# Weights of a convolution interleaved by four columns, and their products written in runs of 8 bytes

## The chip, the cores and the metric

One core of a Trainium2 chip. The metric is device time of one execution in microseconds (us), as a median over runs. Kernels are compared only within the same rounds.

## The reference, cut to what matters

Two independent blocks, concatenated: an attention block A and a long convolution B.

```python
# A: qkv = x @ wqkv, 32 heads of 16; softmax(q k^T * 16**-0.5) @ v; @ wo     (S = 2048, D = 512)
# B: per channel d (512 channels, 2048 positions):
k_shift = sum over t of k_pad[:, t:t + S, :] * shift_k[:, ks - 1 - t]        # 4 taps
kv      = k_shift * v                                                        # <- the products of this case
y       = causal convolution of kv with ssm_k (length S), done by FFT + kv * ssm_D
b       = q * y
```

The kernel does B's long convolution on TensorE: `kv` is the stationary operand (the weights), shifted rows of `ssm_k` are streamed. Two channels share the 128 rows (64 each), and four such pairs run side by side in four column groups of 32.

## The kernel before: the parts that matter

```python
KVF = sb("KV", [128, C // 2, 2, 2 * NB])                 # 256 columns u; 2 parities; 32 weights, contiguous
KV = KVF[:, :, :, :].rearrange("p u r (e h) -> p r e h u", h=2)
...
# one unit "kv": 32 matmuls in two halves into one PSUM bank (L360), then VectorE empties it with two products (L399)
for p in range(2):
    dst = KV[64 * p:64 * p + 64, i // 4, 4 * (i % 4):4 * (i % 4) + 4, p, 128 * c:128 * c + 128]
    val = VST[64 * p:64 * p + 64, c, i // 4, 4 * (i % 4):4 * (i % 4) + 4, :]
    src = PS[64 * p:64 * p + 64, bank, :].rearrange("p (b d) -> p b d", b=4)
    h_kvc[c] = hh = urgent(lambda e, dst=dst, src=src, val=val: e.tensor_tensor(dst, src, val, ALU.mult),
                           [h, h_vn[2 * c + i // 4], h_kv0], us=V512)
bank_free[bank] = hh                                     # the next unit's matmuls wait for the second product
...
# the convolution (L814): for each of 32 lags, four column groups
for c in range(4):
    ins = e.matmul(PS[32 * c:32 * c + 32 - 2 * q, BGB, 128 * kk:128 * kk + w],
                   lhsT=KVF[:, 4 * od + c, lag % 2, 2 * q:32],       # 2 to 32 weights, side by side
                   rhs=WR[:, rows[c], w0:w0 + w], start=(n == 0), stop=(n == NLAG - 1), tile_position=(0, 32 * c))
```

Around this runs the attention. For each score step, TensorE makes two or three blocks of scores (L546), ScalarE exponentiates them (L557), and VectorE takes over one of the three blocks of some steps (L593, L600, L605: some 3.4 us of work each). TensorE also sums with the values (L639). Program order is fixed on each engine before anything runs: of the 13388 matmuls in the traces before and after, 13314 stand at the same place in the order of start. There are 741 score steps with a ScalarE exponential. Below, "step n" is the n-th of them in a trace, so the same piece of work can be found in every trace.

The softmax here doesn't subtract the row's maximum and nothing guards it: scores larger than these inputs give would overflow.

## Time and profile before

1052.42 us (median of 2 runs, 1052.06 to 1052.78). The profiled run lasted 1056.7 us.

| view of the kernel before | value |
|---|---|
| busy share of TensorE, VectorE, ScalarE | 81%, 81%, 81% |
| products L399: number, mean, sum | 32, 2444 ns, 78.2 us |
| share of L399 in the chain that ended last | 7.4% of 1054.9 us, so 78 us |
| stage of the products, steps 60 to 180 (84.7 to 293.4 us): length, mean PE clock | 208.7 us, 0.65 |

Three engines at 81% say little: the share is an average over stages with different limits. The row to read is the third: a group's whole busy time lies on the chain. The lines themselves stand in the prediction.

### The profile page before, as it was taken

The page shows a single profiled execution, that of the slowest core. Times are in us where ns is not written, and L with a number is a line of the kernel's source. Part 1 is how long each engine was busy: PE and PEld are TensorE (multiplying, and loading weights), DVE is VectorE, ACT ScalarE, POOL GpSimd, SP SyncE. Part 2 cuts the span into 40 slices and gives each one's busy share as a digit, 9 for nine tenths or more (in the row PEclk, how much of TensorE's full clock was granted, in tenths as well). Part 3 has the DMA queues.
Part 4 walks back from the last instruction along what each step waited for, and adds up shares of the span by engine and source line. Part 5 has one row for each costly group of instructions (what it writes and reads, how often), then busy time and mean ns, then how long its engine had stood idle before and what let it go on. Part 6 is the DMA issues. An engine that isn't in the chain of part 4 may idle for free.

```text
span 1054.9 us, 29610 instructions
## 1 busy us (share of the span) xinstructions
PE 854.8 (81%) x13388; PEld 333.1 (32%) x13388; DVE 851.4 (81%) x1330; ACT 858.4 (81%) x746; POOL 31.1 (3%) x34
## 2 busy tenths in 40 slices
PE   7987786887788788888788888897788878888877
PEld 2222222233233333333333333333333333333322
DVE  3239898898888798888797968788798879898892
ACT  5896674765598898888797978788799869898897
POOL 7000000000000000000000000000000000000000
PEclk9897585866589898899898978779999879898899
DMA  9940001321498798898787888978778778788602
GB/s 252 246 85 1 1 1 40 81 46 37 103 198 197 164 202 187 197 195 191 155 187 175 185 176 199 235 170 194 168 179 183 163 166 183 178 185 177 139 2 60
DMA packets 68013, 155.14 MB, mean 147 GB/s; under 512 B 31152, under 2 KB 33200, under 8 KB 67504
## 3 DMA queue, kind: packets, MB, share of 16 engines
q1 hardware_dynamic: 62624, 145.12, 62.6%
q0 software_dynamic: 1808, 6.29, 2.1%
q8 instruction: 106, 1.74, 0.8%
q10 hardware_dynamic: 3456, 1.84, 0.6%
q14 instruction: 19, 0.16, 0.1%
HBM read 142.61 MB, written 6.42 MB: 141 GB/s over the span
## 4 chain that ended last, share of the span: by engine, by line
PE 37%; ACT 31%; DVE 21%; issue 8%; DMA 2%; SPq 1%; ACTq 0%; DVEq 0%
ACT PT L557 31%; PE PS L546 13%; PE PS L639 8%; PE PS L814 8%; DVE KV L399 7%; DVE EH L600 6%; DVE FX L593 3%; PE PS L360 2%; DVE PTD L605 2%; DMA WR<-kz_scratch 2%; PE PS L339 2%; PE PS L1019 1%; PE PS L756 1%; SPq L222 1%; DVE DT L703 1%
## 5 line engine op out<-in xcount | busy, mean ns | idle before, releaser
L557 ACT ACTIVATE PT<-PS 128x1536 bf16<-128x1536 f32 (+1 forms) x741 | 855.3, 1269 | 183.9 <-PE PS L546 180.5
L546 PE MATMUL PS<-QT,KTo 32*128 32x512 bf16 x2048 | 347.0, 436 | 85.0 <-ACT PT L557 43.7
L814 PE MATMUL PS<-WR,KV 128*30 128x128 bf16 (+8 forms) x8192 | 265.1, 237 | 47.5 <-issue 40.7
L600 DVE SCALAR_TENSOR_TENSOR EH<-EH,FX 128x512 f32<-128x512 f32 x426 | 280.5, 678 | 0.4
L639 PE MATMUL PS<-PT,VAF 128*32 128x512 bf16 x1835 | 233.4, 443 | 17.4 <-DVE DT L703 8.0
L814 PEld LDWEIGHTS PS<-WR,KV 128*18 128x18 bf16 (+7 forms) x8192 | 173.9, 97 | 157.7 <-issue 125.9
L593 DVE TENSOR_SCALAR FX<-PS 128x512 f32<-128x512 f32 x213 | 145.9, 685 | 70.6 <-PE PS L546 69.9
L546 PEld LDWEIGHTS PS<-QT,KTo 32*128 32x128 bf16 x2048 | 75.1, 93 | 279.5 <-ACT PT L557 158.6
L605 DVE SCALAR_TENSOR_TENSOR PTD<-EH,FX 128x512 uint16<-128x512 f32 x213 | 143.6, 678 | 0.2
L600 DVE SCALAR_TENSOR_TENSOR EH<-FX 128x512 f32<-128x512 uint16 x213 | 141.5, 681 | 0.1
L639 PEld LDWEIGHTS PS<-PT,VAF 128*32 128x32 bf16 x1835 | 51.0, 95 | 163.5 <-issue 140.8
L1019 PE MATMUL PS<-IDN,ZW 128*32 128x512 bf16 (+3 forms) x243 | 83.4, 343 | 4.1 <-issue 4.1
L399 DVE TENSOR_TENSOR KV<-PS,WR 64x512 bf16<-64x512 f32 x32 | 78.2, 2444 | 8.5 <-PE PS L360 8.0
L639 PE MATMUL PS<-PTD,VAF 128*32 128x512 bf16 x213 | 71.5, 448 | 2.2 <-issue 2.2
L703 DVE STREAM_TRANSPOSE DT<-PS 128x512 f32<-128x512 f32 x31 | 22.1, 712 | 32.6 <-PE PS L639 32.4
L412 DVE CAST VAF<-PS 128x512 bf16<-128x512 f32 x16 | 11.1, 691 | 31.7 <-PE PS L368 31.7
L385 DVE TENSOR_SCALAR QT<-PS,MASK 128x512 bf16<-128x512 f32 x30 | 21.1, 745 | 14.6 <-PE PS L339 14.4
L1019 PEld LDWEIGHTS PS<-IDN,ZW 128*32 128x32 bf16 x243 | 25.2, 104 | 8.9 <-issue 8.9
L339 PE MATMUL PS<-xT,WQ 128*128 128x512 bf16 x60 | 24.6, 507 | 3.1 <-DVE KV L399 2.2
L360 PE MATMUL PS<-OTN,QN 128*64 128x128 bf16 x256 | 14.9, 285 | 13.6 <-DVE KV L399 13.5
L360 PE MATMUL PS<-OTN,QT 128*64 128x128 bf16 x256 | 14.9, 285 | 12.7 <-DVE KV L399 12.6
L368 PE MATMUL PS<-WKV,xT 128*128 128x512 bf16 x64 | 21.1, 424 | 4.4 <-DVE VAF L412 4.0
(63 smaller groups left out, 237.1 us busy)
## 6 DMA issues: line engine op xcount, KB each, us to landing
WR<-kz_scratch SPq DMA_DIRECT2D x256, 512.0 KB, 8.7
kz_scratch<-WR SPq DMA_DIRECT2D x1, 2176.0 KB, 8.5
WR<-in_B_v_dram SPq DMA_DIRECT2D x8, 256.0 KB, 6.9
QN<-in_B_q_dram POOLq DMA_DIRECT2D x2, 1024.0 KB, 9.9
out_dram<-QN POOLq DMA_DIRECT2D x2, 1024.0 KB, 10.0
out_dram<-OUTA POOLq DMA_DIRECT2D x12, 128.0 KB, 5.3
QN<-in_B_ssm_k_dram SPq DMA_DIRECT2D x1, 1024.0 KB, 6.3
QT<-in_B_ssm_k_dram SPq DMA_DIRECT2D x1, 1024.0 KB, 8.2
```

Source lines behind the costliest of these rows:

```text
L339: return e.matmul(PS[:, bank, :], lhsT=WQ[:, dc, o * 128:(o + 1) * 128], rhs=xT[:, dc, qb * 512:(qb + 1) * 512], start=(dc == 0), stop=(dc ...
L360: ins = e.matmul(PS[64 * h:64 * h + 64, bank, 128 * b:128 * b + 128], lhsT=KTR[c][:, h, c0:c0 + 64], rhs=DG[:, 2 * c + h, m, :], start=(m ...
L399: h_kvc[c] = hh = urgent(lambda e, dst=dst, src=src, val=val: e.tensor_tensor(dst, src, val, ALU.mult), [h, h_vn[2 * c + i // 4], h_kv0], ...
L546: ins = e.matmul(PS[:, bank, :], lhsT=KTo[32 * s:32 * s + 32, g // 2, kt * 128:(kt + 1) * 128], rhs=QT[32 * s:32 * s + 32, qb % 2, g, :], ...
L557: h_exp[T] = act.op(lambda e: e.activation(PT[:, T % R_PT, 0:n * QB], PS[:, banks[0]:banks[0] + n, :].rearrange("p b f -> p (b f)"), ACT.E ...
L593: h_f = urgent(lambda e: e.tensor_scalar(fx, PS[:, bank, :], FIX_ADD, FIX_HI, ALU.add, ALU.min), [h, h_last.get(i - R_FX)], slack=0.6)
L600: st["h"] = dve.op(lambda e: e.scalar_tensor_tensor(eh, src, (A3, A2, A1)[j], frac, ALU.add, ALU.mult), [st["h"], h_last.get(i - R_EH), h_ ...
L605: lambda e: e.scalar_tensor_tensor(out16, eh, A4, fx, ALU.mult, ALU.add),
L639: ins = e.matmul(dst, lhsT=w, rhs=rhs, start=(k == 0), stop=(k == KT - 1), tile_position=(0, 32 * s))
L703: h_t = urgent(lambda e: e.transpose(out=dt, in_=PS[:, pvb(n), :]), [h] + before, slack=0.1, us=(0.63, 0.751))
L814: ins = e.matmul(PS[32 * c:32 * c + 32 - 2 * q, BGB, 128 * kk:128 * kk + w], lhsT=KVF[:, 4 * od + c, lag % 2, 2 * q:32], rhs=WR[:, rows[c] ...
L1019: pe.op(lambda e: e.matmul(PS[32 * s:32 * s + 32, pvb(n), 0:128 * k], lhsT=ZW[:, :], rhs=rhs, start=False, stop=False, tile_position=(0, 3 ...
```

## The change

The intent: no two consecutive elements of a product were neighbours in memory, so put four channels' columns next to each other and let the product write four of them in a row. The price is that the weights of one load then lie 8 bytes apart.

```diff
-    KVF = sb("KV", [128, C // 2, 2, 2 * NB])
-    KV = KVF[:, :, :, :].rearrange("p u r (e h) -> p r e h u", h=2)
+    KVF = sb("KV", [128, NOCT, 2, 2 * NB, 4])
+    KV = KVF[:, :, :, :, :].rearrange("p k r (e h) c -> p r e h k c", h=2)
 ...
-                dst = KV[..., p, 128 * c:128 * c + 128]
-                val = VST[...]
-                src = PS[64 * p:64 * p + 64, bank, :].rearrange("p (b d) -> p b d", b=4)
+                dst = KV[..., p, 32 * c:32 * c + 32, :].rearrange("p e k c -> p k e c")
+                val = VST[...].rearrange("p e (k c) -> p k e c", c=4)
+                src = PS[64 * p:64 * p + 64, bank, :].rearrange("p (e k c) -> p k e c", e=4, c=4)
 ...
-                                   lhsT=KVF[:, 4 * od + c, lag % 2, 2 * q:32],
+                                   lhsT=KVF[:, od, lag % 2, 2 * q:32, c],
```

("[...]" marks a cut: the indices there are those of before. The zero fill of the tile also got its fifth index.)

More of the change, by code (lines that the diff above doesn't have):

```diff
@@ L313, in bass_concat_heads__mha_block__ssm_conv_h3__prompt_kernel @@
     h_vaf1 = pool.op(lambda e: e.memset(VAF[:, :, H * VW:VROW], 1.0))
-    h_kv0 = pool.op(lambda e: e.memset(KVF[:, :, :, :], 0.0), [h_vaf1], us=(14.0, 14.1))
+    h_kv0 = pool.op(lambda e: e.memset(KVF[:, :, :, :, :], 0.0), [h_vaf1], us=(14.0, 14.1))
     h_kz0 = pool.op(lambda e: e.memset(KZS[:, :, S:S + PAD], 0.0), [h_kv0])
@@ L395, in evac_unit @@
             for p in range(2):
-                dst = KV[64 * p:64 * p + 64, i // 4, 4 * (i % 4):4 * (i % 4) + 4, p, 128 * c:128 * c + 128]
-                val = VST[64 * p:64 * p + 64, c, i // 4, 4 * (i % 4):4 * (i % 4) + 4, :]
-                src = PS[64 * p:64 * p + 64, bank, :].rearrange("p (b d) -> p b d", b=4)
+                dst = KV[64 * p:64 * p + 64, i // 4, 4 * (i % 4):4 * (i % 4) + 4, p, 32 * c:32 * c + 32, :].rearrange("p e k c -> p k e c")
+                val = VST[64 * p:64 * p + 64, c, i // 4, 4 * (i % 4):4 * (i % 4) + 4, :].rearrange("p e (k c) -> p k e c", c=4)
+                src = PS[64 * p:64 * p + 64, bank, :].rearrange("p (e k c) -> p k e c", e=4, c=4)
                 h_kvc[c] = hh = urgent(lambda e, dst=dst, src=src, val=val: e.tensor_tensor(dst, src, val, ALU.mult),
```

## The prediction

> **What bounds the kernel now.** I read four views: the groups by line (what the changed instruction costs), the chain of waits (whether that cost sets the end), that line's own view (who waits for it), and the busy times by stage (what could take its place).
>
> The groups by line, of the page; the columns are busy us and mean ns, then the idle time ahead and what ended it:
>
> ```profile
> L399 DVE TENSOR_TENSOR KV<-PS,WR 64x512 bf16<-64x512 f32 x32 | 78.2, 2444 | 8.5 <-PE PS L360 8.0
> L412 DVE CAST VAF<-PS 128x512 bf16<-128x512 f32 x16 | 11.1, 691 | 31.7 <-PE PS L368 31.7
> ```
>
> L399 writes the conv's weights, 512 elements per partition, in 2444 ns. L412, equally long and also from PSUM into bf16, takes 691 ns. The one thing that sets L399 apart is where it writes: consecutive elements land one column (64 bf16, 128 bytes) apart. Its excess is (2444 - 691) x 32 = 56 us.
>
> The chain that ended last, by line, says that none of it is hidden:
>
> ```profile
> by line: ACT PT L557 31.0%; PE PS L546 13.4%; PE PS L639 8.1%; issue 7.7%; PE PS L814 7.5%; DVE KV L399 7.4%; DVE EH L600 5.5%; DVE FX L593 2.6%; PE PS L360 2.0%; DVE PTD L605 1.9%; DMA WR<-kz_scratch 1.7%; PE PS L339 1.7%; PE PS L1019 1.4%
> ```
>
> 7.4% of 1054.9 us is 78 us: all 32 instructions, end to end. The chain in order of time, between 146 and 179 us, shows the loop (start us, length us, what):
>
> ```profile
> 151.46 0.64 PE PS L360 x16
> 152.10 0.96 PE PS L546 x3
> 153.06 0.55 PE PS L639 x4
> 153.61 0.96 PE PS L546 x2
> 154.57 1.01 PE PS L360 x16
> 155.61 2.45 DVE KV L399
> 158.08 2.45 DVE KV L399
> 160.58 1.06 PE PS L360 x16
> ```
>
> A unit is two groups of L360 matmuls into one PSUM bank and two L399 products that empty it. There is one such bank, TensorE works in program order, and so the next unit, and every attention score queued behind it, waits for both products. The line's own view says so too:
>
> ```profile
> who waited for it (us, times):
>   PEld PS L360: 30.5, 10
>   PE PS L360: 26.1, 10
> ```
>
> The stages hold all of L399 (88 to 276 us). Columns: us, busy us of PE, PEld, DVE, ACT, POOL with counts, PE clock, DMA share, GB/s; the last row is the steady part without L399:
>
> ```profile
> 84.00:115.00 31.00, 22.25 (x190) 7.75 (x189) 28.41 (x29) 20.13 (x19) 0.00 (x0) 0.61 0.00 1
> 115.00:146.00 31.00, 26.05 (x199) 7.73 (x199) 27.75 (x42) 22.74 (x22) 0.00 (x0) 0.73 0.00 1
> 146.00:179.00 33.00, 19.02 (x190) 7.52 (x186) 29.46 (x26) 15.52 (x15) 1.32 (x1) 0.64 0.10 25
> 179.00:207.00 28.00, 25.84 (x279) 7.84 (x267) 24.20 (x39) 24.38 (x23) 0.00 (x0) 0.80 0.27 63
> 207.00:278.00 71.00, 50.92 (x647) 22.24 (x647) 65.43 (x62) 38.41 (x35) 0.00 (x0) 0.62 0.19 40
> 430.00:1030.00 600.00, 492.82 (x9059) 204.11 (x9056) 513.38 (x865) 519.74 (x444) 7.76 (x12) 0.88 0.78 172
> ```
>
> In the steady part ScalarE is the fullest engine (87%). In 207 to 278 it is at 54% while VectorE is at 92%, and the PE clock falls to 0.62: there VectorE bounds the kernel, by L399.
>
> [...] 2444/512 = 4.8 ns per element here, with 2-byte elements 128 bytes apart. [...] L847, a `tensor_tensor` of 512 elements with an operand in PSUM, has a median of 682 ns. [...]
>
> **The change part by part.**
>
> Added or removed instructions: none. The program order on all five engines is that of before; only L399's access patterns and the source of L814's weights differ. The zero fill of the weight tile is the same contiguous size.
>
> *The products.* Destination: runs of 4 bf16, then a hop of 16 or 512 bytes. The WR operand: runs of 8 bytes. The PSUM operand: runs of four fp32 (16 bytes), hops of 2 KiB inside one bank. [...] Hops in PSUM cost nothing already: L847 reads its PSUM operand at a stride and takes 682 ns, L828 reads it backwards in 680. I take 690 ns, so 32 x 1.75 = **56 us** leave VectorE and, at first, the chain.
>
> *The weight loads.* 8192 loads in L814, 2 to 32 columns each. In the trace one lasts 79 to 97 ns at full clock, growing by 0.45 ns per column. Four go out 4 ns apart, one set of products ahead; the median period of a set is 56 ns for 2 columns as for 20, so the 128 streamed columns set it and not the loads. If spaced columns load at the old rate, nothing changes. If they took twice as long, a lone load would grow by at most 32 x 0.45 = 14 ns, behind the set ahead. Only if the four also share one read path would sets of over 16 columns stretch (4 x 32 x 0.9 = 115 ns against 56): on average some 25 ns on half of the 2048 sets, **26 us** of PE, perhaps half of it on the path. I give that one chance in eight.
>
> *What of the 56 us stays.* Stage by stage I take off 1.75 us for each L399 begun there and then ask what share ScalarE would have to reach (at 100% it binds):
> - 84 to 115 (6 of them): 31 - 10.5 = 20.5 us, ACT 20.1: nearly full. I keep 8.5.
> - 115 to 146 (3): 25.8 us, ACT 88%. I keep 5.
> - 146 to 179 (8): 19 us, ACT 82%. I keep 13.
> - 179 to 207 (the tail of the last, little to gain): 1.5.
> - 207 to 278 (15): 44.8 us, ACT 86%, DVE (65.4 - 26.3)/44.8 = 87%. I keep 23.
>
> Sum **51 us**. ScalarE's share in the steady part is the reason to think 82 to 88% attainable. PE is the doubt: its 50.9 us in the last stage don't fit 44.8 us at a clock of 0.62. But with 4.9 us holes gone it should be granted more; at 0.75 the same work is about 42 us. After 278 us ScalarE already sets the pace and no instruction there becomes cheaper, so I expect that part only to start earlier.
>
> 1052.4 - 51 = **1001 us**.
>
> **The rivals.**
> - *The clock stays low.* Then TensorE replaces VectorE as the bound in the stages: 50.9 us in 207 to 278 gives back 6, 146 to 179 holds at 19 as predicted, and 84 to 146 gives back perhaps 4. For it: clock 0.61 to 0.73 there, and 115 to 146 is cold with few products. Against it: the holes that L399 makes are most of PE's idle time. Time: about 1011.
> - *The clock rises well.* TensorE's cold pieces on the chain (0.96 where a warm one takes 0.54 us) shrink as well, worth up to 10 us beyond the 56 less what ScalarE caps. Time: about 990.
> - *The loads become the bound.* Conv weight loads slow down through 178 to 1027 us and eat 13 to 26 us. For it: nothing in the trace measures a spaced load. Against: [...] the slack in the set period. Time: 1014 to 1027.
> - *The products get faster only in part*, say 1.2 us, because an operand hops on both sources and the destination at once. Saving 40 us of busy time, about 36 of the end: 1016.
> - *A transfer catches up.* The conv rows come by DMA, 96% busy from 278 to 330 us. A shorter first part leaves less time to fetch; but slots, not bandwidth, limit it before (share 0.19 in 207 to 278). A few us at most.
>
> **Range and chances.** The first two rivals set the middle of the range, 990 to 1011; the others widen it upwards slightly. Range 989 to 1014. "Within 2%" (above 1031) needs slowed loads together with a poor product, or a slowed clock on top: 5%. Slower by over 2% needs loads several times slower: 1%.
>
> **What would show it.** L399 near 690 ns, about 22 us in all, and no more than 2% of the chain. TensorE's waits for it down from some 26 us on L360 to under 8. In 84 to about 225 us, ScalarE above 80% and a clock above 0.7. A load of 32 columns still near 97 ns, period of a set 56 ns. L557's total unchanged at 855 us. The time from the end of the last L399 to the end of the kernel unchanged, near 778 us, to within 5. I am wrong if L399 stays over 1 us, if loads lengthen with the period of a set, or if the rest after L399 grows.

Three assumptions stand as what they were, estimates. That a product writing four elements in a row takes 690 ns rests on L412 (691 ns) and L847 (682 ns), which write rows of 16 elements. That spaced columns load at the old rate rests on nothing in the trace, as no load of the kernel before is spaced. That a clock with fewer holes is higher was only seen side by side there (0.62 in 207 to 278 us, 0.88 in the steady part); e3_fill_before and e6_fill_fit tested it (from 0.65 to 0.81 and 0.77 in the stage).

## The result, and the profile after

981.51 us (median of 2 fast runs, 979.65 to 983.38). The ratio is 0.9326, 95% interval 0.925 to 0.940. A second timing, among the experiments (e11_after), gave 0.931. The time lies below the predicted range.

The group of the products, of the page after; busy us and mean ns follow the bar:

```profile
L399 DVE TENSOR_TENSOR KV<-PS,WR 64x512 bf16<-64x512 f32 x32 | 21.9, 686 | 6.1 <-PE PS L360 5.5
```

That is the predicted 690 ns. Who waited for it, after:

```profile
  PEld PS L360: 2.8, 5
  PE PS L360: 1.2, 3
```

TensorE's waits of 26.1 us for the products ahead of L360 have gone to 1.2 us. The chain in order of time shows the same pieces of the program as the first lines of the prediction's fence that begins at 151.46 (start us, length us, what):

```profile
131.28 0.64 PE PS L360 x16
131.91 0.54 PE PS L546 x3
132.45 0.33 PE PS L639 x4
132.78 0.53 PE PS L546 x2
133.31 0.59 PE PS L360 x16
133.90 0.02 issue
133.92 0.68 DVE KV L399
134.61 0.03 issue
134.64 0.71 DVE KV L399
```

Two things are different here, not one. The product is 0.7 us in place of 2.45. And each piece of TensorE's but the first is shorter too: the same three scores take 0.54 us where they took 0.96, the second half unit 0.59 where it took 1.01, although not one of these instructions was changed. All five pieces run at full clock now (granted clock 1.00 in each); before, only the first did (0.98, and 0.50 in the other four).

To see what that is worth I cut both traces at the same score steps, so that each row holds the same work. The columns are the stretch, its length, then the busy us of PE, PEld, DVE, ACT and POOL with counts, the mean PE clock, DMA share and GB/s. Before, for steps 60 to 78, 78 to 100, 100 to 113, 113 to 136, 136 to 170 and 170 to 180:

```profile
84.65:116.75 32.10, 23.29 (x209) 8.59 (x205) 29.45 (x31) 19.52 (x20) 0.00 (x0) 0.59 0.00 1
116.75:146.74 29.99, 25.10 (x184) 6.88 (x180) 26.80 (x40) 23.44 (x23) 0.00 (x0) 0.75 0.00 1
146.74:179.89 33.15, 19.17 (x193) 7.60 (x196) 29.61 (x26) 14.83 (x15) 1.32 (x1) 0.63 0.12 31
179.89:210.81 30.92, 26.64 (x288) 8.65 (x284) 26.71 (x40) 24.45 (x24) 0.00 (x0) 0.78 0.32 70
210.81:278.21 67.40, 49.44 (x632) 21.29 (x628) 62.08 (x60) 38.34 (x35) 0.00 (x0) 0.63 0.16 34
278.21:293.38 15.17, 15.17 (x128) 3.98 (x124) 10.98 (x18) 10.86 (x11) 0.00 (x0) 0.50 1.01 221
```

And after, the same steps:

```profile
81.96:106.21 24.25, 22.73 (x209) 8.56 (x205) 19.89 (x32) 19.56 (x19) 0.00 (x0) 0.64 0.01 2
106.21:129.99 23.78, 21.91 (x184) 6.70 (x184) 22.09 (x39) 22.88 (x22) 0.00 (x0) 0.94 0.00 1
129.99:145.30 15.31, 12.14 (x193) 5.46 (x195) 14.91 (x25) 14.20 (x14) 1.32 (x1) 1.00 0.04 6
145.30:169.79 24.49, 23.69 (x289) 8.01 (x293) 23.72 (x40) 23.65 (x23) 0.00 (x0) 0.93 0.40 100
169.79:210.79 41.00, 36.20 (x636) 17.49 (x632) 36.97 (x60) 36.49 (x35) 0.00 (x0) 0.88 0.33 70
210.79:220.96 10.17, 9.15 (x128) 3.09 (x124) 10.10 (x18) 10.17 (x11) 0.00 (x0) 1.00 0.92 207
```

| steps | before | after | saved | foreseen in the prediction |
|---|---|---|---|---|
| 60 to 78 | 32.1 | 24.2 | 7.9 | 8.5 |
| 78 to 100 | 30.0 | 23.8 | 6.2 | 5 |
| 100 to 113 | 33.1 | 15.3 | 17.8 | 13 |
| 113 to 136 | 30.9 | 24.5 | 6.4 | 1.5 |
| 136 to 170 | 67.4 | 41.0 | 26.4 | 23 |
| 170 to 180 | 15.2 | 10.2 | 5.0 | 0 |
| sum | 208.7 | 139.0 | 69.7 | 51 |

The last row is the most telling. No product stands in it in either kernel, and it holds the same 128 matmuls. Before, TensorE is busy for all 15.17 us at a clock of 0.50: it is the bound. After, the clock is 1.00, and ScalarE is busy for all 10.17 us. Why the clock stayed at 0.50 in this row is not shown: TensorE had no gap from 276.5 us on, and the clock rose only at 295.4. Holes further ahead do not settle it either. With the slow products of e3_fill_before (below) the row ahead had a clock of 0.82 and this one again 15.2 us at 0.50; in e2_three_half the row ahead had 0.67 and this one 11.2 us at 0.90. Outside steps 60 to 180 the two profiles differ by 7 us (2.7 ahead of step 60, 4.7 behind step 180). In kernels with this order the part from step 180 to the start of the last score step takes 744 to 760 us whatever the product, so nothing is to be explained there.

The chain by line over steps 60 to 180, before and then after:

```profile
by line: DVE KV L399 37.4%; PE PS L546 14.1%; PE PS L360 10.3%; DVE EH L600 8.6%; PE PS L639 8.4%; DVE FX L593 4.0%; PE PS L339 3.6%; DVE PTD L605 2.6%; PE PS L814 2.5%; DVE KTo L390 2.3%; issue 2.3%; PE PS L348 1.6%; DVE QT L385 0.7%; DVE 
```

```profile
by line: ACT PT L557 20.1%; DVE EH L600 13.9%; PE PS L546 13.8%; PE PS L360 8.8%; DVE KV L399 8.6%; DVE FX L593 7.5%; PE PS L639 7.3%; DVE PTD L605 5.3%; issue 2.9%; DVE KTo L390 2.6%; PE PS L814 1.9%; DVE DT L703 1.5%; PE PS L1019 1.5%; PE
```

In us (share times length of the part): the products fall from 78.1 to 12.0. L546, L360, L639 and L814 of TensorE together fall from 35.3% of 208.7 to 31.8% of 139.0, so from 73.7 to 44.2 us. ScalarE, not among the groups of before, comes in with 27.9 us. So more left the chain than the products, and only part of it was taken over by another engine.

### The profile page after: what moved, and what is told of

The parts are those of the page before. It is cut to its first block, busy times and chain, and to the rows that moved or that the text cites. A ratio compares the mean times of both kernels' runs of the same rounds, so it can differ in the third digit from the quotient of the medians.

```text
span 977.8 us, 29610 instructions
## 1 busy us (share of the span) xinstructions
PE 813.6 (83%) x13388; PEld 329.1 (34%) x13388; DVE 792.9 (81%) x1330; ACT 851.5 (87%) x746; POOL 31.5 (3%) x34
## 4 chain that ended last, share of the span: by engine, by line
ACT 37%; PE 32%; DVE 20%; issue 9%; SPq 1%; DMA 1%; ACTq 0%
ACT PT L557 37%; PE PS L546 12%; DVE EH L600 8%; PE PS L814 8%; PE PS L639 7%; DVE FX L593 4%; DVE PTD L605 3%; PE PS L1019 1%; PE PS L360 1%; DVE KV L399 1%; PE PS L339 1%; DVE DT L703 1%; DVE QT L385 1%; SPq L222 1%; DMA WR<-in_B_ssm_D_dram 1%
## 5 line engine op out<-in xcount | busy, mean ns | idle before, releaser
L557 ACT ACTIVATE PT<-PS 128x1536 bf16<-128x1536 f32 (+1 forms) x741 | 848.5, 1279 | 113.9 <-PE PS L546 111.6
L546 PE MATMUL PS<-QT,KTo 32*128 32x512 bf16 x2048 | 330.8, 416 | 83.1 <-ACT PT L557 44.1
L814 PE MATMUL PS<-WR,KV 128*30 128x128 bf16 (+8 forms) x8192 | 262.0, 234 | 46.0 <-issue 44.4
L639 PE MATMUL PS<-PT,VAF 128*32 128x512 bf16 x1835 | 222.1, 422 | 14.7 <-issue 8.2
L814 PEld LDWEIGHTS PS<-WR,KV 128*18 128x18 bf16 (+7 forms) x8192 | 175.5, 99 | 150.1 <-issue 117.4
L546 PEld LDWEIGHTS PS<-QT,KTo 32*128 32x128 bf16 x2048 | 74.7, 92 | 264.1 <-ACT PT L557 176.3
L600 DVE SCALAR_TENSOR_TENSOR EH<-FX 128x512 f32<-128x512 uint16 x213 | 142.0, 684 | 0.1
L639 PEld LDWEIGHTS PS<-PT,VAF 128*32 128x32 bf16 x1835 | 50.7, 94 | 151.5 <-issue 132.7
L639 PE MATMUL PS<-PTD,VAF 128*32 128x512 bf16 x213 | 68.7, 432 | 0.0
L412 DVE CAST VAF<-PS 128x512 bf16<-128x512 f32 x16 | 11.1, 691 | 29.2 <-PE PS L368 29.2
L399 DVE TENSOR_TENSOR KV<-PS,WR 64x512 bf16<-64x512 f32 x32 | 21.9, 686 | 6.1 <-PE PS L360 5.5
L222 POOL DMA_DIRECT2D out_dram<-OUTA x12 | 6.6, 547 | 591.8 <-DVE OUTA L765 591.8
L339 PE MATMUL PS<-xT,WQ 128*128 128x512 bf16 x60 | 21.4, 447 | 1.0 <-DVE QN L847 0.9
L756 PE MATMUL PS<-WKV,OTN 128*128 128x512 bf16 x64 | 20.1, 393 | 1.2 <-DVE OTN L725 1.2
```

What stands on the lines that cost most here:

```text
L339: return e.matmul(PS[:, bank, :], lhsT=WQ[:, dc, o * 128:(o + 1) * 128], rhs=xT[:, dc, qb * 512:(qb + 1) * 512], start=(dc == 0), stop=(dc ...
L546: ins = e.matmul(PS[:, bank, :], lhsT=KTo[32 * s:32 * s + 32, g // 2, kt * 128:(kt + 1) * 128], rhs=QT[32 * s:32 * s + 32, qb % 2, g, :], ...
L557: h_exp[T] = act.op(lambda e: e.activation(PT[:, T % R_PT, 0:n * QB], PS[:, banks[0]:banks[0] + n, :].rearrange("p b f -> p (b f)"), ACT.E ...
L600: st["h"] = dve.op(lambda e: e.scalar_tensor_tensor(eh, src, (A3, A2, A1)[j], frac, ALU.add, ALU.mult), [st["h"], h_last.get(i - R_EH), h_ ...
L639: ins = e.matmul(dst, lhsT=w, rhs=rhs, start=(k == 0), stop=(k == KT - 1), tile_position=(0, 32 * s))
```

## The experiments

Theory S: the change is worth the 56 us that leave VectorE, each one for one. Theory C: more, because products on the chain leave TensorE idle, its clock falls, and its own pieces of the loop get longer. Rival B: more, because VectorE as a whole (186 of 209 us busy) bounds the stage, exponentials queued behind slow products included. And what the spaced weight loads cost was open.

All runs gave the reference's result within tolerance. "Stage" is steps 60 to 180, of the one execution that was profiled; times are medians of the fast runs, products a mean or a median.

| run | product, ns | median us | ratio to before (95%) | stage us | PE clock in it |
|---|---|---|---|---|---|
| before (first profile) | 2444 | 1052.4 | | 208.7 | 0.65 |
| b1_before | | 1043.9 | one look | 207.5 | 0.68 |
| changed kernel (first profile) | 686 | 981.5 | 0.933 (0.925 to 0.940) | 139.0 | 0.88 |
| e1_twice | 2 x 690 | 1015.2 | 0.967 (0.961 to 0.973) | 168.1 | 0.78 |
| e2_three_half | 3.5 x 690 | 1057.0 | 1.009 (1.003 to 1.015) | 213.1 | 0.68 |
| e3_fill_before | as before | 1045.6 | 1.000 (0.992 to 1.007) | 207.8 | 0.81 |
| e6_fill_fit | 2440 | 1048.2 | 0.999 (0.990 to 1.009) | 201.0 | 0.77 |
| e10_fill_fit2 | as e6 | 1046.1 | one look | 202.2 | 0.80 |
| e7_no_dve_exp | 2442 | 1039.7 | 0.992 (0.986 to 0.998) | 215.5 | 0.71 |
| e8_no_dve_exp_after | 688 | 966.8 | 0.924 (0.916 to 0.932) | 142.0 | 0.96 |
| e11_after | as changed | 975.7 | 0.931 (0.921 to 0.942) | a slow run | |
| e12_late | as e8 | 964.6 | 0.918 (0.908 to 0.927) | 140.6 | 0.99 |
| e9_natural | 688 | 983.8 | one look | 132.8 | 0.95 |
| e4_runs16 | 688 | 987.7 | 0.942 (0.935 to 0.948) | 131.0 | 0.97 |
| e13_runs4 | 688 | 985.6 | 0.940 (0.932 to 0.949) | 136.2 | 0.91 |
| e14_walk | 1037 | 994.5 | 0.945 (0.939 to 0.950) | 148.5 | 0.86 |
| e15_runs4_late | 689 | 968.6 | 0.919 (0.913 to 0.925) | 143.5 | 0.94 |

### The product made long again, in steps: e1_twice, e2_three_half

```diff
                 h_kvc[c] = hh = urgent(... tensor_tensor(dst, src, val, ALU.mult) ...)       # changed kernel
+                for _ in range(1):                                                           # e1; range(2) in e2
+                    h_kvc[c] = hh = dve.op(... the same product again ..., [hh], us=(0.0, 0.0))
+                h_kvc[c] = hh = dve.op(... its first half ..., [hh], us=(0.0, 0.0))          # e2 only
```

> The changed kernel with every product issued twice, so VectorE spends 0.69 us more on each of the 32 (22 us in all); right result, weights still spaced. Theory S (the product's own length is all there is): 981.5 + 22 = 1003 us. Theory C (each us of product costs more than one, because TensorE's clock falls in the holes): 981.5 + 27 = 1008 us or more, with a lower granted clock between 85 and 230 us. If waits are partly hidden at this length: under 1000.

> As the run before, with the product issued three times and then once at half length: about 2.45 us per product, as long as in the kernel before, but with the weights spaced. If the whole gain comes from the product's length: 1052 us within 4. If the spaced loads cost something that the gain hid: over 1058. If the spaced weights help by themselves: under 1046. Theory S, where 56 us of product cost 56 us, would say 1037.

Measured: 1015 and 1057 us. Here is the stage in e1_twice and in e2_three_half, columns as above:

```profile
83.53:251.68 168.15, 138.16 (x1613) 52.15 (x1613) 150.37 (x241) 129.63 (x121) 1.32 (x1) 0.78 0.20 46
```

```profile
80.98:294.13 213.15, 154.17 (x1613) 56.97 (x1613) 186.47 (x305) 130.93 (x121) 1.32 (x1) 0.68 0.17 37
```

22.7 us more of VectorE (150.4 against 127.7) cost 29 us of the stage, and 58.8 us more cost 74. Theory S is out: each us of VectorE's costs about 1.27 us (1.22 to 1.26 if the gaps between the repeated products are counted in). The clock falls with the length, 0.88, 0.78, 0.68. The second run brings back the whole gain, although its weights stay spaced: 3.5 products take 2.59 us from the first start to the last end, 0.14 us more than the one of before, so 4.6 us over all 32. That is within the 0.3 to 1.5% by which the run lies over before. From step 180 to the last score step, where nearly all of the convolution lies, it takes 750.6 us, against 753.4 and 744.5 us in the kernel before. So the spaced loads cost nothing that shows. By rows the match is less exact: steps 170 to 180 stay 4.0 us shorter than before, and the other rows are 8.4 us longer, of which the product explains 4.6; the rest is not explained.

### TensorE kept busy in the holes: e3_fill_before, e6_fill_fit, e10_fill_fit2, b1_before

```diff
+    def fill_hole(count):     # products of 512 columns with zero weights, added to a live sum: the result stays right
+        ... for _ in range(count): e.matmul(PS[.. a live bank ..], lhsT=ZW, rhs=IDN.., start=False, stop=False)
                 # ahead of the first half of a kv unit, kernel before
+                if u[0] == "kv" and not half: fill_hole(10 unless i % 4 == 0)      # e3
+                if u[0] == "kv" and not half: fill_hole(FILL_KV.get(u[1:], 0))     # e6, e10: 4 to 8
+            fill_hole(FILL_QK.get(T, 0))                                           # e6, e10: 7 to 9 ahead of 3 score steps
```

> The kernel before with its slow products, and ten 512-column products with zero weights put in front of the units that wait for the bank, so that TensorE is busy in the holes and its clock stays up; right result. Theory C (the clock): granted clock between 85 and 290 us up from about 0.65 to over 0.8, time 8 to 14 us below before. Rival B (the gain beyond 56 us is VectorE's backlog, not the clock): clock up, time within 3 us of before, or later where the fill overruns the holes.

The clock went from 0.65 to 0.81, and the time stayed. By the expectation Theory C had lost. But the chain showed the fill itself: 8.1 us of it (3.9% of the stage), and at one place the ten zero products took 4.38 us at half clock while the VectorE product that they were to hide behind had already ended, at 261.1 us:

```profile
262.56 4.38 PE PS L1037 x10
```

A fill that overruns its hole proves nothing, so I sized it to each hole in the trace of before.

> The kernel before once more, with the zero-weight products now sized to each hole that its trace shows ahead of TensorE (4 to 9 of 512 columns, also ahead of three score products), so that they end inside the hole even at half clock; right result. Theory C (the clock in the holes costs the excess over 56 us): the part from score step 60 to 180 falls from 209 us to 190 to 200 at a clock over 0.85, and the time by 10 to 18 us. Rival B (the excess is VectorE's queue, the clock is only a companion): the clock rises and that part stays above 204 us.

> The fitted fill again, unchanged. Theory C: steps 60 to 180 again some 6 to 10 us shorter than in the kernel before of the same call, at a clock 0.1 higher. Rival: within 3 us of it.

> The kernel before again, for the scatter of the part from score step 60 to 180 between executions: 209 us at a clock of 0.65 in its first profile. If that part scatters by 8 us or more, the 201 us that the fitted fill showed mean nothing.

Measured: the stage took 201.0 and 202.2 us, against 208.7 and 207.5 us without fill. The looks at the same kernel agree within 1.2 us, so the 6.5 us are more than the scatter seen, on two executions of each kernel. The stage of e6_fill_fit:

```profile
84.68:285.65 200.97, 159.54 (x1683) 58.16 (x1683) 185.16 (x209) 129.41 (x121) 1.32 (x1) 0.77 0.20 44
```

VectorE's busy time is that of before, so this is not its work but TensorE's clock. It falls short of the expected 190 to 200 us, and the whole time doesn't resolve it (ratio 0.999, interval of 2%). The row of steps 170 to 180 gained nothing: 15.2 us at a clock of 0.50 in both fitted fills. So the clock is a cause of the excess, by this edit in the rows ahead of step 170. TensorE's pieces get shorter, and the products of 78 us stay on the chain.

The other direction needs no edit. Four kernels have the same instructions in the same order with a product of 686 to 688 ns: the changed one, e13_runs4, e9_natural and e4_runs16. Their stages took 139.0, 136.2, 132.8 and 131.0 us at clocks of 0.88, 0.91, 0.95 and 0.97. That is 8.0 us for about 0.1, seen side by side and not set by an edit. As an estimate, the two slopes (6.5 us for 0.12, 8.0 for 0.1) make the rise from 0.65 to 0.88 worth 12 to 18 us. The excess to be explained is 69.7 us saved less the 57.9 that VectorE did less (185.6 - 127.7), so 11.8 us. The changed kernel's profile is the slowest of these four; against 131.0 us the saving and the excess would be 8 us larger.

### VectorE's other work taken out of the stage: e7_no_dve_exp, e8_no_dve_exp_after

```diff
-T_DVE = 56
+T_DVE = 172          # e7: kernel before; e8: changed kernel
```

> The kernel before with VectorE's share of the exponentials begun only at step 172 in place of 56, so that slow products stand alone in VectorE's queue; some 29 blocks go to ScalarE, about 12.5 us of it. Rival B (VectorE's total work in that part, 186 us of 209, bounds it): steps 60 to 180 fall by 15 us or more, below 194. Theory L (the loop of product, bank and next unit bounds it, whatever else VectorE does): that part stays at 200 or more.

> The changed kernel with the same late start of VectorE's exponentials. ScalarE then holds 127 + 12.5 = 139.5 us in steps 60 to 180, so if ScalarE is what is left after the change, that part takes 142 to 152 us against 139, and the whole 3 to 12 us more than the changed kernel; if VectorE (128 of 139 us) is what is left, the part gets shorter, 125 to 135 us is then not possible as ScalarE alone takes 139.5, so it would stay at 139 to 141.

The stage, with the slow product and with the fast one:

```profile
85.59:301.11 215.52, 158.83 (x2058) 63.20 (x2058) 112.50 (x87) 140.54 (x122) 1.32 (x1) 0.71 0.32 72
```

```profile
83.00:225.01 142.01, 126.91 (x2058) 52.79 (x2058) 56.56 (x88) 135.78 (x122) 1.32 (x1) 0.96 0.50 113
```

In e7_no_dve_exp VectorE does 73 us less (112.5 against 185.6) and is half idle, and yet 75.9 of the 78 us of products are still on the stage's chain:

```profile
by line: DVE KV L399 35.2%; ACT PT L557 21.0%; PE PS L360 13.4%; PE PS L546 10.7%; PE PS L639 5.5%; issue 3.8%; PE PS L339 3.7%; PE PS L348 3.4%; PE PS L814 3.1%; PE PS L1019 0.3%; PE PS L839 0.2%
```

So what binds there is the loop of unit, product and bank, not VectorE's load. That its stage is not shorter (215.5 us) says nothing by itself: it holds 2058 matmuls in place of 1613, because the schedule brought convolution forward, and the span from the first product to the last did shrink, from 188 to 159 us, with fewer score steps in it. The pair e7 and e8, with one schedule, decides: without any queue of exponentials, 56 us of product less make 73.5 us of stage less, the clock from 0.71 to 0.96. Rival B is out as the cause of the excess.

Against what I expected, e8_no_dve_exp_after as a whole was not slower but faster than the changed kernel: its stage gives away 3 us or more, and behind step 180 it takes 728.5 us in place of 748.7, because convolution was done earlier. So I timed the two side by side:

> The changed kernel again, beside the next. 980 to 988 us; steps 60 to 180 in 131 to 139 us, the shorter the higher the clock (about 8 us per 0.1).

> The changed kernel with VectorE's exponentials begun at step 172, again, timed beside the changed kernel on one chip: 967 us, 12 to 18 us below the changed kernel, if the first result was no accident; within 4 us of it otherwise.

The ratios are 0.931 and 0.918, and their intervals still touch (0.921 to 0.942, 0.908 to 0.927); the first pair gave 0.933 and 0.924. Two of the four runs of e11_after were slow. Its two fast ones took 973.3 and 978.1 us, those of e12_late 955.0 to 965.2. So this version beats the kernel before, and it is probably some 1.4% faster than the changed one, which the intervals don't settle. The profile of e11_after fell in a slow run, so its stage isn't used.

### Spacing of the weights, width of the runs: e4_runs16, e13_runs4, e9_natural, e14_walk, e15_runs4_late

```diff
-    KVF = sb("KV", [128, NOCT, 2, 2 * NB, 4])          # changed kernel; the other indices follow
+    KVF = sb("KV", [128, 32, 2, 2 * NB, 8])            # e4: runs of 16 bytes, columns 16 bytes apart
+    KVF = sb("KV", [128, 128, 2, 2 * NB, 2])           # e13: runs of 4 bytes; e15: the same and T_DVE = 172
     # e9: changed layout, product walked "p e k c" in place of "p k e c" (both sources contiguous)
     # e14: layout of before, dst, val and src walked "p d e" in place of "p e d"
```

> The changed kernel with eight columns interleaved: products in runs of 16 bytes, weight columns 16 bytes apart[...]. Product still 0.69 us. [...] If the four loads of a set run side by side, the period of a set stays 56 ns and the time within 5 us of 981.5; if they share one path, wide sets stretch and the time grows by 10 to 25 us.

> The changed kernel with two columns interleaved: products in runs of 4 bytes[...], and weight columns 4 bytes apart; right result. [...] product between 0.9 and 1.5 us. If any adjacent pair of elements were enough: 0.69 us and the time of the changed kernel. With a product of 1.2 us the line through the measured points (0.69 us: 139 us, 1.38 us: 168 us) gives steps 60 to 180 about 160 us and the whole 1003 us. A load of 32 columns between 96 and 108 ns.

> The changed kernel with the product walked in the order of its sources: both sources read without hops, the destination still in runs of 8 bytes. If hops on the sources cost nothing: product 690 ns as in the changed kernel. If they cost: under 670 ns. One look, so its time only says 975 to 995.

> The kernel before with its own weight layout, and the product only walked in another order: the four blocks innermost, so that it writes single bf16 elements 4 bytes apart, [...] then hops 128 bytes; both sources hop on every element. Rule A (elements must be adjacent): 2 us or more, time near the kernel before. Rule B [...]: near 0.69 us and about 984 us. In between: 1.2 us, about 1010 us.

> Two columns interleaved (product 0.69 us, loads as fast as contiguous ones) together with VectorE's exponentials begun at step 172: 960 to 968 us, some 18 us below the changed kernel, of which almost all is the late start; steps 60 to 180 near 140 us, ScalarE over 95% busy in them.

The product's line in e13_runs4 and in e14_walk (min/median/max ns):

```profile
L399 DVE TENSOR_TENSOR KV<-PS,WR x32: 668/688/696, 85.8 to 206.3; 64x512 bf16<-64x512 f32 x32
```

```profile
L399 DVE TENSOR_TENSOR KV<-PS,WR x32: 1021/1037/1065, 88.5 to 220.3; 64x512 bf16<-64x512 f32 x32
```

Two neighbours are enough for the 688 ns of the changed kernel's layout, against what I expected, and eight (e4_runs16, 688 ns) bring no more than two. Hops of the sources between such runs cost nothing here: e9_natural, without any, has the same 688 ns. Single elements 4 bytes apart, written four at a time, cost 1037 ns, and single elements 128 bytes apart 2444 ns. Of the two rules that I set against each other, A foresaw 2 us or more and B 0.69 us; the 1037 ns fit neither. Single elements cost more than pairs (1037 against 688 ns), and the far ones much more (2444). But e14_walk also makes both sources hop on every element, where before read them without hops; what of its 1037 ns is the destination's was not separated. It touches no layout at all and brings some four fifths of the gain with three reordered patterns (994.5 us, ratio 0.945 where the changed kernel has 0.933). At 1.04 us the product costs 9.5 us of stage against the 139.0 us of the changed kernel and 17.5 against the 131.0 of e4_runs16, for 11.7 us of VectorE, so whether part of it is hidden at this length stays open.

The weight loads, line L814 (min/median/max ns over all 8192), of before, the changed kernel, e4_runs16 and e13_runs4:

```profile
L814 PEld LDWEIGHTS PS<-WR,KV x8192: 79/90/151, 178.5 to 1027.2; 128*6 128x6 bf16 x15, 128*32 128x32 bf16 x14, 128*14 128x14 bf16 x14, 128*26 128x26 bf16 x14
```

```profile
L814 PEld LDWEIGHTS PS<-WR,KV x8192: 78/95/152, 144.4 to 950.1; 128*6 128x6 bf16 x15, 128*14 128x14 bf16 x14, 128*32 128x32 bf16 x13, 128*2 128x2 bf16 x13
```

```profile
L814 PEld LDWEIGHTS PS<-WR,KV x8192: 81/112/165, 140.0 to 953.1; 128*6 128x6 bf16 x15, 128*32 128x32 bf16 x14, 128*14 128x14 bf16 x14, 128*26 128x26 bf16 x14
```

```profile
L814 PEld LDWEIGHTS PS<-WR,KV x8192: 79/90/151, 141.8 to 949.1; 128*6 128x6 bf16 x15, 128*32 128x32 bf16 x14, 128*14 128x14 bf16 x14, 128*24 128x24 bf16 x13
```

Columns 4 bytes apart load like contiguous ones (median 90 ns in both); 8 bytes apart they are slower (95), 16 bytes apart slower still (112). Sorted by width at full clock, a load of 32 columns takes 95, 96, 107 and 137 ns at 2, 4, 8 and 16 bytes; one of 2 columns takes 84 or 85 ns in all four. The median period of a set of four is 56 ns at every width with 2, 4 and 8 bytes (57 at 30 columns). With 16 bytes it rises to 84 ns at 30 columns and 67 at 32: there the spaced loads begin to show in the period. Even so e4_runs16 isn't told apart from the changed kernel in time. Whether the four loads of a set share a path was not shown.

e15_runs4_late is the late start on the layout with the unslowed loads: 968.6 us, ratio 0.919. It is not told apart from e12_late (0.918), so the layout of two adds nothing measurable.

## Why the prediction was wrong

- **Right: what bounds.** That all of L399 was on the chain, through the one bank, is confirmed by e7_no_dve_exp (75.9 us still on the chain with VectorE half idle). "There VectorE bounds the kernel, by L399" holds for L399, and not for VectorE's load as a whole.
- **Right: the product's cost.** 690 ns foreseen, 686 measured; 22 us in sum, 1.2% of the chain; waits on L360 from 26.1 to 1.2 us.
- **Right in effect, wrong in a size: the loads.** I wrote "if spaced columns load at the old rate, nothing changes". They don't: 32 columns grew by 12 ns, nearly the 14 ns given for twice the time per column (I had 0.45 ns per column; sorted by width in the trace of before it is some 0.4, from 84 ns at 2 columns to 95 at 32). The period of a set stayed 56 ns, so it was hidden, as said for that case.
- **Wrong: "What of the 56 us stays."** This is the step that failed. I treated 56 us as the most there was and took 5 off, since ScalarE would reach 82 to 88% and TensorE's clock might stay low. The stage saved 69.7 us. ScalarE reached 127.0 of 139.0 us, 91%. And the clock rose from 0.65 to 0.88, past the 0.75 I reckoned with, which shortened TensorE's own pieces of the loop. That the length of the product does all this is shown by e1_twice and e2_three_half: 58.8 us of VectorE put back cost 74 us of stage.
- **Where the missing 19 us sit.** 4.8 in steps 100 to 113, 4.9 in 113 to 136, 3.4 in 136 to 170 and 5.0 in 170 to 180 (with 1.2 in 78 to 100, and 0.6 too many in 60 to 78). Two of these rows, 113 to 136 and 170 to 180, hold two products and none. I gave them 1.5 and 0, with "After 278 us ScalarE already sets the pace". It did not until 293 us: TensorE did, at a clock of 0.50. The window that I had asked for there, 278 to 330 us, hid this in a mean clock of 0.80. What held the clock down in this row stays open.
- **The right rival, held too small.** "The clock rises well" named the mechanism and gave 990 us. Its error is the clause "less what ScalarE caps": I used ScalarE's share of the steady part as a ceiling. It is only what that part happens to reach. Of the 11.8 us by which the gain exceeds VectorE's saving, the clock explains all by the estimate above (12 to 18 us). What is shown by an edit is 6.5 us for 0.12 of clock; the rest is inference from executions that differed in clock.
- **Also off:** the time from the last product's end to the end of the kernel, foreseen as 778 us within 5, was 768 us (977.8 - 209.6); half of the difference is the row 170 to 180. L557's total was 848.5 us in place of 855.
- **Two misreadings that changed no sum.** I had read a half clock without a break from 101 to 142 us; in the trace it lies from 90.6 to 131.6 us. Within it TensorE's matmuls ran from 103.9 to 113.2 us without a gap, and the clock stayed at 0.50: 9.3 us of unbroken work did not raise it there. The PSUM operand's hops are 512 bytes (128 fp32), not 2 KiB.

## What to carry to other kernels

Two neighbouring bf16 elements in a row took this product from 2444 to 688 ns, and four or eight took it no further: where a writer is strided, try two before looking at anything larger. Check with one reordered access pattern first, as that may give most of it without a change of layout (here e14_walk, ratio 0.945 where the changed kernel has 0.933). When a wait that idles TensorE again and again leaves the chain, count as gain the wait and also what TensorE's own pieces lose in length if the clock rises (here 69.7 us of stage for 57.9 us of VectorE's work, with the mean clock from 0.65 to 0.88), and look at the clock in the stretch just behind the waits too (0.50 before, 1.00 after in steps 170 to 180). A busy share that some other stage reaches is not a ceiling for this one: ScalarE had 87% in the steady part and reached 91% here.
